# A pre-norm layer of linear attention and a gated bilinear block: the query weights' means taken off by GpSimd in place, three loads moved to ScalarE's queue, two key chunks loaded as one

## The chip, the core and the metric

The kernel runs on one core of one Trainium2 chip. The metric is device microseconds from launch to end, as the median of several runs. The core has five engines that work side by side, each with an instruction stream of its own: TensorE (PE; its weight loads are PEld), VectorE (DVE), ScalarE (ACT), GpSimd (POOL) and SyncE (SP). In this kernel SP does nothing but issue DMAs; ScalarE can issue some too.

## The reference

x is 2048 rows of 640 in bf16. LN takes off a row's mean and divides by its standard deviation.

```python
# 32 heads of 20; softmax over the 20 features of a head, once of p and once of -p
h  = x + A(LN(x))
h2 = h + B(LN(h))

# A: q, k, v = LN(x) @ wqkv, split by heads
pq = einsum("bhsd,hdf->bhsf", q, w_phi);  pk = the same of k
phi_q = concat([softmax(pq), softmax(-pq)]);  phi_k = the same of pk
kv = einsum("bhsf,bhsd->bhfd", phi_k, v);  z = sum over s of phi_k
o  = (phi_q @ kv) / (phi_q . z + 1e-6)
A  = o @ wo

# B: F = 1536
B = ((y @ w_gate) * (y @ w_up)) @ w_down        # y = LN(h)
```

## The kernel before

The 2048 rows are 16 tiles of 128; D = 640 is five chunks of 128 (`NC`). Rows sit on partitions. A row's mean is taken off not from x but from the weights, so that a product with raw x equals one with the centred x; the row's scale `rs` comes later, in the exponential or the evacuation.

**Weights.** Wq, Wk, Wv are the thirds of wqkv. The feature map w_phi is folded into Wk and Wq on the chip: Wk (or Wq) is transposed, and chunk i of the folded matrix is the product of the transposed weights `WT` with the block-diagonal `Phi`. For Wk (`wk_rounds`, units `wk` and `x0` to `x4`) the five chunks are loaded one by one into `Wnat` and transposed by TensorE. For Wq, five DMA transposes (`wqT`, units `t0` to `t4`) write `WT[:, 0]` straight from HBM; `Wnat` then takes plain Wq (unit `lwq`), from which `wq_means` (unit `wm`) computes the mean of each row a of `WT` with small matmuls against `ones`. ScalarE spreads minus the means over 128 columns as `nmu`, a tile that lies in the first buffer of `outb`. `wq_round(i)` (units `y0` to `y4`) then adds two products in one PSUM buffer: six matmuls of `WT` with `Phi`, and six of `nmu` with `Phi`. `evac` writes the sum to `Wp`, by ScalarE for even i, by VectorE for odd. The means of Wk of chunks 2 to 4 are taken off while VectorE and ScalarE evacuate the transposes; for chunks 0 and 1 there is a second product with `nmuk` as above.

**Rows.** 16 DMA transposes of x (`load_xT`; the first four belong to unit `in`, the others are `lT4` to `lT15`) bring `xT`. `stats` (units `s0`, `s2`, `s4`, `s8`, `s12` for the tiles 0-1, 2-3, 4-7, 8-11, 12-15) gets the row sums and, up to tile 11, the sums of squares from matmuls of `xT` with itself; GpSimd turns them into `rs`. Then the units per tile t: `k` projects the keys (ten matmuls of 320 columns), VectorE takes the largest magnitude, ScalarE two exponentials; `K` sums by head (VectorE) and multiplies by the reciprocals (GpSimd, 128x1280); `v` projects the values; `q` and `Q` do for the queries what `k` and `K` do for the keys, and two DMA transposes turn the result. `A0` to `A14` gather keys times values over all tiles in one PSUM buffer, `Aout` writes it to `KVsb`; `n` is the numerator and division, `h` the product with Wo and the residual; `f` the gate and up products, `d` and `e` the down product, the residual and the store.

**Order.** Every piece of work is an operation with its engine, its registers (for the dependences) and its buffers, made by `Prog.op`. The order on each engine is written out in `ORDER`: a list of units per engine, each mention taking that unit's next operation on that engine. `place` walks through the five lists with assumed durations to hand out the buffers of the pools (four PSUM buffers of two banks, three for `eq`, two each for the others) and `finish` sets the semaphores. An engine runs its list strictly in order: what waits holds up everything behind it on that engine. DMAs are issued by SP in its list's order, but for Wrows (w_phi), which ScalarE issues first of all.

Of the kernel before, what the change touches and what calls it, by code (L numbers as in the profile page):

```python
# [5 lines left out]
FP32 = mybir.dt.float32  # L6
# [5 lines left out]
P = 128  # L12
# [60 lines left out]
    "DVE":  # L73
# [12 lines left out]
    "ACT":  # L86
# [9 lines left out]
    "POOL":  # L96
# [37 lines left out]
class Op:  # L134
    __slots__ = ("eng", "idx", "emit", "deps", "dma", "waits", "vc", "signal", "tick", "sem", "val",
                 "n", "dur", "lat", "bufs", "succ", "start", "end", "open", "bytes", "unit")


class Prog:
# [13 lines left out]
    def op(self, eng, emit, rd=(), wr=(), app=(), dma=None, t=0.2, lat=None, use=(), after=(), size=0.0):  # L153
        o = Op()
        o.eng, o.emit, o.dma = eng, emit, dma
# [44 lines left out]
    def place(self):  # L200
# [20 lines left out]
        while len(order) < len(ops):  # L221
# [29 lines left out]
            if o.dma is not None:  # L251
                land = max(s + 2.3, fabric) + o.bytes
                fabric = land
                o.end = land + o.lat
                flight.setdefault(o.dma[0], []).append(o.end)
            else:
                o.end = s + o.lat
# [119 lines left out]
def _build(ctx, nc, A_x, A_wqkv, A_w_phi, A_wo, B_w_gate, B_w_up, B_w_down, out):  # L377
# [43 lines left out]
    nmean = sb([P, NC], FP32, "nmean")  # L421
    Ssum = sb([P, 2, 2 * H], FP32, "Ssum")
# [9 lines left out]
    nmu, nmuk = [outb[:, k, :].rearrange("p (a n) -> p a n", a=NC) for k in range(2)]  # L432
# [31 lines left out]
    def load(out_, in_, wr, mb, after=(), eng="SP", app=()):  # L464
        return g.op(eng, lambda e: e.dma_start(out_, in_), wr=wr, app=app, after=after, dma=("w", 8), t=0.5, lat=0.4, size=mb / 0.38)  # L465

    def transpose(out_, in_, rd, wr, use=(), t=1.27, size=1.07):

        return g.op("SP", lambda e: e.dma_start_transpose(out_(), in_()), rd=rd, wr=wr, use=use, dma=("tr", 8), t=t, lat=0.5,  # L469
                    size=size)  # L470
# [27 lines left out]
    def load_wnat(w, cs=(0, NC), eng="SP"):  # L498
        c0, c1 = cs
        load(Wnat[:, c0:c1, :], A_wqkv[P * c0:P * c1, D * w:D * (w + 1)].rearrange("(c p) n -> p c n", p=P), R_Wnat[c0:c1],  # L500
             0.16 * (c1 - c0), eng=eng)

    def load_xT(t):
        transpose(lambda: xT[:, t, :, 0:P], lambda: A_x[0, P * t:P * (t + 1), :], [], [R_xT[t]], t=1.27, size=0.8 if t < 2 else 1.4)

    def load_x(b):
        load(x_all[:, 4 * b:4 * b + 4, :], A_x[0, 4 * P * b:4 * P * (b + 1), :].rearrange("(t p) n -> p t n", p=P), [R_x[b]], 0.64)

    def load_wv(c0, c1):
        load(Wp[:, c0:c1, 2 * D:3 * D], A_wqkv[P * c0:P * c1, 2 * D:3 * D].rearrange("(c p) n -> p c n", p=P), R_Wp[2][c0:c1], 0.16 * (c1 - c0))  # L510

    U("in")
    load(Wrows[:, :, :], A_w_phi.rearrange("h d f -> (h d) f").rearrange("(a p) f -> p a f", p=P), [R_Wrows], 0.03, eng="ACT")
    for c in range(NC):
        load_wnat(1, (c, c + 1))
    load_wv(0, 2)
# [587 lines left out]
```

## Time and profile before

| | us |
|---|---|
| median of 3 runs (lowest to highest) | 281.2 (280.83 to 281.42) |
| the profiled execution | 281.24 |
| its span, first to last instruction | 279.4 |
| busy: PE, PEld | 274.6, 187.7 |
| busy: DVE, ACT, POOL | 165.5, 133.4, 106.3 |
| DMA: 28.08 MB in 65241 packets | mean 100 GB/s |

The granted TensorE clock is full throughout. Times in the views are microseconds from the start of the span; "x10" behind a group counts its instructions; a bracket "[0.55 <-DVE ...]" is idle time ahead of an instruction and what ended it. L568 is the helper that issues all matmuls, L469 the DMA transposes on SP's queue (SPq), L465 the plain loads, L827 and L857 GpSimd's products of keys and queries, L686 its spreading of Wk's means. The share of the DMA engines counts the time of packets, those that wait included, so that it can exceed 1.

### The profile page before, as it was taken

The numbers are of one execution on the slowest core, as the hardware profiler recorded it, in microseconds if no ns is written. First come the engines' busy times: TensorE is split into PE (matmuls) and PEld (weight loads), VectorE is DVE, ScalarE is ACT, GpSimd is POOL, SyncE is SP. The second block draws the span as 40 slices with busy tenths as digits, with TensorE's granted clock in tenths as the row PEclk, the third lists the DMA queues.
The fourth block names the chain that finished last, engine by engine and source line by source line (L and its number), as shares of the span: only waits on it lengthen the run. The fifth ranks groups of instructions, "written<-read, shape, count | busy, mean of one in ns | idle before, by whom it ended". The sixth has DMA issues, their size and how long they took to land.

```text
span 279.4 us, 5540 instructions
## 1 busy us (share of the span) xinstructions
PE 274.6 (98%) x2257; PEld 187.7 (67%) x2257; DVE 165.5 (59%) x313; ACT 133.4 (48%) x227; POOL 106.3 (38%) x156
## 2 busy tenths in 40 slices
PE   8999999999999999999999999999999999999996
PEld 7777778778878888877746655676454444456773
DVE  2999999999899798688528474431141132315011
ACT  2477999998566346363271432401444342410321
POOL 5348899999620322233300680002521034000321
PEclk9999999999999999999999999999999999999999
DMA  7989989404964378946530065561210001000112
GB/s 192 166 170 140 214 125 397 137 2 94 302 78 94 74 180 150 280 99 91 122 73 2 7 136 72 116 98 45 72 49 0 0 0 49 0 0 2 70 48 72
DMA packets 65241, 28.08 MB, mean 100 GB/s; under 512 B 55744, under 2 KB 63936, under 8 KB 65216
## 3 DMA queue, kind: packets, MB, share of 16 engines
q1 hardware_dynamic: 64560, 27.70, 45.8%
q8 instruction: 18, 0.29, 0.5%
q10 hardware_dynamic: 656, 0.03, 0.2%
q14 instruction: 7, 0.06, 0.1%
HBM read 11.82 MB, written 2.62 MB: 52 GB/s over the span
## 4 chain that ended last, share of the span: by engine, by line
PE 94%; SPq 3%; DMA 2%; DVE 1%; issue 0%
PE ps L568 93%; SPq L469 2%; DMA xT<-in_A_x_dram 2%; SPq L465 1%; PE ps L480 0%; DVE outb L1010 0%; DVE KVsb L893 0%; DVE rden L927 0%; DVE KVsb L896 0%
## 5 line engine op out<-in xcount | busy, mean ns | idle before, releaser
L568 PE MATMUL ps<-phik,Wgu 128*128 128x512 bf16 (+1 forms) x600 | 107.6, 336 | 0.0
L568 PEld LDWEIGHTS ps<-phik,Wgu 128*128 128x128 bf16 x600 | 58.2, 98 | 43.6 <-DVE phik L969 1.2
L969 DVE TENSOR_TENSOR phik<-ps,gate 128x512 bf16<-128x512 f32 (+1 forms) x60 | 34.0, 575 | 61.2 <-PE ps L568 60.3
L568 PE MATMUL ps<-Wp,xT 128*128 128x320 bf16 x480 | 68.4, 299 | 0.0
L967 ACT ACTIVATE gate<-ps 128x512 bf16<-128x512 f32 (+1 forms) x60 | 30.1, 512 | 70.4 <-PE ps L568 56.5
L568 PE MATMUL ps<-vaug,phik 128*128 128x320 bf16 (+3 forms) x544 | 60.2, 270 | 0.0
L568 PEld LDWEIGHTS ps<-Wp,xT 128*128 128x128 bf16 x480 | 46.2, 98 | 17.1
L568 PEld LDWEIGHTS ps<-vaug,phik 128*128 128x128 bf16 x544 | 43.4, 97 | 15.9
L985 POOL TENSOR_TENSOR outb<-t,x_all 128x640 bf16<-128x640 f32 x12 | 16.8, 1397 | 88.0 <-ACT t L982 85.7
L827 POOL TENSOR_TENSOR phik<-phik,Rk 128x1280 bf16<-128x1280 bf16 x16 | 37.3, 2357 | 0.7 <-DVE nb L809 0.6
L982 ACT ACTIVATE t<-ps,mh,rs 128x640 f32<-128x640 f32 x12 | 10.6, 882 | 41.4 <-PE ps L568 41.4
L806 DVE TENSOR_REDUCE ps<-ps 128x1 f32<-128x640 f32 x32 | 26.2, 819 | 3.5 <-PE ps L568 3.1
L846 DVE TENSOR_REDUCE Sq<-eq 128x64 f32<-128x1280 bf16 x16 | 23.5, 1474 | 1.6 <-ACT eq L813 1.6
L824 DVE TENSOR_REDUCE Ssum<-phik 128x64 f32<-128x1280 bf16 x16 | 23.4, 1471 | 0.1
L857 POOL TENSOR_TENSOR eq<-eq,rq 128x640 bf16<-128x640 bf16 x16 | 20.3, 1270 | 0.9
L852 POOL TENSOR_TENSOR rq<-Sq,rq 128x32 f32<-128x32 f32 x16 | 4.0, 255 | 39.8 <-DVE rq L851 39.8
L813 ACT ACTIVATE eq<-ps,nb,rs 128x640 bf16<-128x640 f32 x16 | 14.1, 883 | 10.1 <-DVE nb L809 9.3
L813 ACT ACTIVATE phik<-ps,nb,rs 128x640 bf16<-128x640 f32 x16 | 14.0, 884 | 3.1 <-DVE nb L809 3.0
L561 ACT ACTIVATE junk<-x_all 128x640 bf16<-128x640 bf16 x20 | 14.7, 735 | 0.0
L833 ACT ACTIVATE vaug<-ps,rs 128x640 bf16<-128x640 f32 x16 | 12.8, 801 | 3.5 <-PE ps L568 3.5
L813 ACT ACTIVATE eq<-ps,nb,nrs 128x640 bf16<-128x640 f32 x16 | 14.1, 882 | 0.0
L946 DVE SCALAR_TENSOR_TENSOR x_all<-ps,mh,x_all 128x640 bf16<-128x640 f32 x16 | 13.9, 874 | 0.4
(83 smaller groups left out, 226.4 us busy)
## 6 DMA issues: line engine op xcount, KB each, us to landing
x_all<-in_A_x_dram SPq DMA_DIRECT2D x4, 640.0 KB, 9.0
out_dram<-outb SPq DMA_DIRECT2D x15, 160.0 KB, 1.8
Wgu<-in_B_w_up_dram SPq DMA_DIRECT2D x1, 1920.0 KB, 11.3
Wgu<-in_B_w_gate_dram SPq DMA_DIRECT2D x1, 1920.0 KB, 8.2
vaug<-in_B_w_down_dram SPq DMA_DIRECT2D x1, 1920.0 KB, 8.5
phiqT<-in_A_wqkv_dram SPq DMA_DIRECT2D x5, 160.0 KB, 3.8
phiqT<-in_A_wqkv_dram SPq DMA_DIRECT2D x1, 800.0 KB, 6.0
Wo<-in_A_wo_dram SPq DMA_DIRECT2D x1, 800.0 KB, 5.6
```

Of the source, the lines that this page charges most:

```text
L561: g.op("ACT", lambda e: e.activation(out=junk[:, v.i, :], in_=in_, func=func, accum_out=acc), rd=rd, wr=wr, use=[v], t=0.73, lat=0.97)
L568: ins = e.matmul(o_, lhsT=l_, rhs=r_, start=s_, stop=p_, skip_group_check=True)
L806: g.op("DVE", lambda e: e.tensor_reduce(out=mx(), in_=PS[v.i][:, :, 0:HALF], axis=AX.XY, op=ALU.max, apply_absolute_value=True, negate=Tru ...
L813: g.op("ACT", lambda e, s=s, sc=sc: e.activation(out=signed(dst(), s), in_=PS[v.i][:, :, 0:HALF].rearrange("p b (h f) -> p b h f", f=DH), ...
L824: g.op("DVE", lambda e: e.tensor_reduce(out=Ssum[:, vs.i, :], in_=x, axis=AX.X, op=ALU.add), rd=R_phik[t], wr=vs.R, use=[vs], t=1.39, lat=1.5)
L827: g.op("POOL", lambda e: e.tensor_tensor(out=x, in0=x, in1=Rk[:, vr.i, :].unsqueeze(2).to_broadcast([P, 2 * H, DH]), op=ALU.mult), rd=vr.R ...
L846: g.op("DVE", lambda e: e.tensor_reduce(out=Sq[:, vs.i, :], in_=eq[:, b.i, :].rearrange("p (g f) -> p g f", f=DH), axis=AX.X, op=ALU.add), ...
L857: return e.tensor_tensor(out=x, in0=x, in1=rq[:, vr.i, :].unsqueeze(2).to_broadcast([P, H, DH]), op=ALU.mult)
L946: g.op("DVE", lambda e: e.scalar_tensor_tensor(out=xv, in0=PS[v.i][:, :, 0:HALF], scalar=mh[:, t:t + 1], in1=xv, op0=ALU.subtract, op1=ALU ...
L967: g.op("ACT", lambda e: e.activation(out=gate[:, vg.i, 0:P * n], in_=PS[v.i][:, 0, 0:P * n], func=ACT.Copy), rd=[v.R[0]], wr=vg.R, use=[v, ...
L969: g.op("DVE", lambda e: e.tensor_tensor(out=hhT[:, hb, ft, sl], in0=PS[v.i][:, 1, 0:P * n], in1=gate[:, vg.i, 0:P * n], op=ALU.mult), rd=[ ...
L985: g.op("POOL", lambda e: e.tensor_tensor(out=outb[:, vo.i, :], in0=t32[:, v3.i, :], in1=x_all[:, t, :], op=ALU.add), rd=v3.R + [R_h[t]], w ...
```

## The change

It has three parts and a new `ORDER`.

- `wq_means` writes minus the five means as 128x5 (`nmeanq`) on ScalarE, and five GpSimd instructions (units `wq0` to `wq4`) add column a to `WT[:, 0, a, :]` in place; `wq_round` drops the six matmuls with `nmu`.
- Wq (`lwq`), Wo (`lwo`) and the last quarter of x (`lx3`) are issued by ScalarE: `lx3` and `lwq` behind the evacuation of x4, `lwo` behind `wm`.
- Chunks 2 and 3 of Wk are one load of 320 KB, issued by ScalarE behind Wrows; chunks 0, 1 and 4 stay with SP.
- The lists of all five engines are written anew. Assumed durations in `place` change as well (`at`, `t`, `size`, `lat`); they act on the hand-out of buffers and DMA semaphores alone.

```diff
 ORDER, heads of the lists
 "PE":
-  warm wk x10 x1 wv x1 x0 x3 wv x0 s0 s0 x2 x4 k0 k0 k0 s2 k0 k0 s2 k1 k3 v1 k2 s4 s4 s4 s4
-  k6 k4 v5 k7 v6 k5 v3 s8 s8 s8 s8 k8 v4 wm v11 k9 v10 k10 s12 v7 s12 s12 s12 y4 y0 y1 y3 k11 y2 ...
+  warm wk x10 x1 wv x1 x3 x0 x0 wv s0 x2 k0 s0 k0 x4 k0 k0 s2 k1 s2 k0 k3 s4 s4 s4 s4
+  k6 v0 k4 wm k5 v7 v3 k2 s8 s8 s8 s8 k7 v5 v2 y4 k8 s12 s12 y0 s12 s12 k9 y1 v4 y3 k11 y2 ...
+  ... k15 v9 A0 v13 A2 q2 A2 q3 v15 A4 A4 q5 A6 A6 A8 A8 A10 A12 A14 A10 A12 A14 n0 n1 n1 q6 n1 n0 q7 n0 ...
 "ACT":
-  in wk wk wk in x0 x2 x4 k0 k0 k1 v1 k1 k3 k3 k2 s12 k2 v5 k4 k4 ...
+  in in in wk wk wk x0 x2 x4 lx3 lwq k1 k1 k0 k0 k3 k3 v0 s12 wm lwo k6 k6 s12 v7 k4 v3 k4 ...
 "POOL":
-  ... s4 K1 K0 K3 s8 s8 s8 s8 s8 s8 K2 K4 K6 s12 K5 K8 s12 ...
+  ... s4 s2 K1 wq1 wq2 K3 K0 wq4 s8 wq0 wq3 s8 s8 s8 s8 s8 K5 s4 s12 K6 s12 ...
 "SP":
-  in x11 lT4 lT5 lT7 lT6 lx3 lT8 lT11 lT10 lT9 lT15 t0 lT13 lwq t3 lT12 t2 t4 t1 lT14 lwo lu lx0 lx2 Q0 Q0 ...
+  in x9 lT4 lT6 lT5 lT7 t1 t2 lT8 lT11 lT10 lT9 t3 t4 lT15 t0 lT13 lT12 lT14 lg lx0 lu Q0 Q0 lx2 ...
...
-    for c in range(NC):
-        load_wnat(1, (c, c + 1))
+    load_wnat(1, (0, 1), at=3.0)
+    load_wnat(1, (2, 4), "ACT", at=4.8)
+    load_wnat(1, (1, 2), at=3.7)
+    load_wnat(1, (4, 5), at=5.3)
...
-        g.op("ACT", lambda e: e.activation(out=nmu[:, :, :], in_=PS[v.i][:, 0, 0:NC].unsqueeze(2).to_broadcast([P, NC, P]),
-                                           func=ACT.Copy, scale=-1.0 / SC), rd=[v.R[0]], wr=[R_nmu], use=[v], t=0.61, lat=0.75)
+        g.op("ACT", lambda e: e.activation(out=nmeanq[:, :], in_=PS[v.i][:, 0, 0:NC], func=ACT.Copy, scale=-1.0 / SC),
+             rd=[v.R[0]], wr=[R_nmu], use=[v], t=0.1, lat=0.23)
+        for a in range(NC):
+            U("wq%d" % a)
+            pool_op(lambda e, a=a: e.tensor_scalar(out=WT[:, 0, a, :], in0=WT[:, 0, a, :], scalar1=nmeanq[:, a:a + 1], scalar2=None,
+                                                   op0=ALU.add), 0.75, rd=[R_nmu, R_WT[0][a]], wr=[R_WT[0][a]])
...
-        g.op("PE", lambda e: mms(e, part(WT[:, 0, :, P * i:P * (i + 1)], first) + part(nmu, first)), rd=R_WT[0] + R_Phi + [R_nmu],
-             wr=v.R, use=[v], t=0.62, lat=0.77)
+        g.op("PE", lambda e: mms(e, part(WT[:, 0, :, P * i:P * (i + 1)], first)), rd=R_WT[0] + R_Phi,
+             wr=v.R, use=[v], t=0.31, lat=0.46)
...
-    load_wnat(0)
+    load_wnat(0, eng="ACT")
...
-    load(Wo[:, :, 0:D], A_wo.rearrange("(c p) n -> p c n", p=P), R_Wo, 0.8)
+    load(Wo[:, :, 0:D], A_wo.rearrange("(c p) n -> p c n", p=P), R_Wo, 0.8, eng="ACT")
```

In the heads of the lists "wk x10" and "in x9" count mentions in a row.

More of the change, by code (lines that the diff above doesn't have):

```diff
@@ L135 @@
     __slots__ = ("eng", "idx", "emit", "deps", "dma", "waits", "vc", "signal", "tick", "sem", "val",
-                 "n", "dur", "lat", "bufs", "succ", "start", "end", "open", "bytes", "unit")
+                 "n", "dur", "lat", "bufs", "succ", "start", "end", "open", "bytes", "unit", "at")
 class Prog:
@@ L151, in __init__, with op @@
         self.order = {}
-    def op(self, eng, emit, rd=(), wr=(), app=(), dma=None, t=0.2, lat=None, use=(), after=(), size=0.0):
+    def op(self, eng, emit, rd=(), wr=(), app=(), dma=None, t=0.2, lat=None, use=(), after=(), size=0.0, at=0.0):
         o = Op()
+        o.at = at
         o.eng, o.emit, o.dma = eng, emit, dma
@@ L251, in place @@
             if o.dma is not None:
-                land = max(s + 2.3, fabric) + o.bytes
+                land = o.at or max(s + 2.3, fabric) + o.bytes
                 fabric = land
@@ L421, in _build @@
     nmean = sb([P, NC], FP32, "nmean")
+    nmeanq = sb([P, NC], FP32, "nmeanq")
     Ssum = sb([P, 2, 2 * H], FP32, "Ssum")
@@ L431, in _build @@
     WT = pq[:, NC * D:3 * NC * D].rearrange("p (w a n) -> p w a n", w=2, a=NC)
-    nmu, nmuk = [outb[:, k, :].rearrange("p (a n) -> p a n", a=NC) for k in range(2)]
+    nmuk = outb[:, 1, :].rearrange("p (a n) -> p a n", a=NC)
     vaug = BV[:, :].rearrange("p (t h e) -> p t h e", t=NT, h=H)
@@ L462, in _build, with load, transpose @@
     R_hT, R_oT, R_hhT = [regs(4) for _ in range(2)], [regs(4) for _ in range(2)], [[regs(4) for _ in range(NF)] for _ in range(2)]
[L464 to L470, printed above, removed]
+    def load(out_, in_, wr, mb, eng="SP", at=0.0):
+        return g.op(eng, lambda e: e.dma_start(out_, in_), wr=wr, dma=("w", 8), t=0.5, lat=0.4, size=mb / 0.38, at=at)
+    def transpose(out_, in_, rd, wr, use=(), t=1.27, size=1.07, lat=0.5, at=0.0):
+        return g.op("SP", lambda e: e.dma_start_transpose(out_(), in_()), rd=rd, wr=wr, use=use, dma=("tr", 8), t=t, lat=lat,
+                    size=size, at=at)
     def transpose_pe(out_, in_, rd, wr, use, v, bk):
@@ L494, in U, with load_wnat, load_xT, load_wv @@
         g.unit = name
-    def load_wnat(w, cs=(0, NC), eng="SP"):
+    def load_wnat(w, cs=(0, NC), eng="SP", at=0.0):
         c0, c1 = cs
         load(Wnat[:, c0:c1, :], A_wqkv[P * c0:P * c1, D * w:D * (w + 1)].rearrange("(c p) n -> p c n", p=P), R_Wnat[c0:c1],
-             0.16 * (c1 - c0), eng=eng)
-    def load_xT(t):
-        transpose(lambda: xT[:, t, :, 0:P], lambda: A_x[0, P * t:P * (t + 1), :], [], [R_xT[t]], t=1.27, size=0.8 if t < 2 else 1.4)
+             0.16 * (c1 - c0), eng=eng, at=at)
+    def load_xT(t, at=0.0):
+        transpose(lambda: xT[:, t, :, 0:P], lambda: A_x[0, P * t:P * (t + 1), :], [], [R_xT[t]], t=1.3, size=0.75, lat=1.25, at=at)
     def load_x(b):
-        load(x_all[:, 4 * b:4 * b + 4, :], A_x[0, 4 * P * b:4 * P * (b + 1), :].rearrange("(t p) n -> p t n", p=P), [R_x[b]], 0.64)
-    def load_wv(c0, c1):
-        load(Wp[:, c0:c1, 2 * D:3 * D], A_wqkv[P * c0:P * c1, 2 * D:3 * D].rearrange("(c p) n -> p c n", p=P), R_Wp[2][c0:c1], 0.16 * (c1 - c0))
+        load(x_all[:, 4 * b:4 * b + 4, :], A_x[0, 4 * P * b:4 * P * (b + 1), :].rearrange("(t p) n -> p t n", p=P), [R_x[b]], 0.64,
+             eng="ACT" if b == NB - 1 else "SP")
+    def load_wv(c0, c1, at):
+        load(Wp[:, c0:c1, 2 * D:3 * D], A_wqkv[P * c0:P * c1, 2 * D:3 * D].rearrange("(c p) n -> p c n", p=P), R_Wp[2][c0:c1], 0.16 * (c1 - c0), at=at)
     U("in")
-    load(Wrows[:, :, :], A_w_phi.rearrange("h d f -> (h d) f").rearrange("(a p) f -> p a f", p=P), [R_Wrows], 0.03, eng="ACT")
-    for c in range(NC):
-        load_wnat(1, (c, c + 1))
-    load_wv(0, 2)
-    load_wv(2, 5)
-    for t in range(4):
-        load_xT(t)
+    load(Wrows[:, :, :], A_w_phi.rearrange("h d f -> (h d) f").rearrange("(a p) f -> p a f", p=P), [R_Wrows], 0.03, eng="ACT", at=3.3)
+    load_wnat(1, (0, 1), at=3.0)
+    load_wnat(1, (2, 4), "ACT", at=4.8)
+    load_wnat(1, (1, 2), at=3.7)
+    load_wnat(1, (4, 5), at=5.3)
+    load_wv(0, 2, 6.6)
+    load_wv(2, 5, 8.5)
+    for t, at in enumerate((7.9, 8.5, 10.3, 11.5)):
+        load_xT(t, at)
     def pool_op(f, t, **k):
@@ L1019, in wqT @@
         U("t%d" % a)
-        transpose(lambda: WT[:, 0, a, :], lambda: A_wqkv[:, P * a:P * (a + 1)], [], [R_WT[0][a]], t=1.27, size=1.4)
+        transpose(lambda: WT[:, 0, a, :], lambda: A_wqkv[:, P * a:P * (a + 1)], [], [R_WT[0][a]], t=1.5, size=0.75, lat=1.25)
     U("warm")
```

86 rows, old and new, of the table ORDER are left out of this document.

## The prediction

> **What bounds the kernel now.** I read the chain of waits first, then TensorE's timeline, then the queue that issues DMAs, then GpSimd's groups. The chain of work that ended last, in order of time:
>
> ```profile
> 3.60 0.47 SPq L465
> 4.07 0.04 issue
> 4.12 1.30 SPq L469
> ...
> 9.02 4.64 DMA xT<-in_A_x_dram
> 13.65 0.05 issue
> 13.70 62.00 PE ps L568 x670
> ...
> 76.62 1.91 PE ps L568 x20
> ...
> 85.88 190.10 PE ps L568 x1312
> ```
>
> Up to 13.70 us the end hangs on issues and on the fourth transposed tile of x; from there it is TensorE to 275.99 us, with one gap of 0.55 us before 76.62 (waiting for KVsb). After it 3.4 us of evacuation and store remain. So whatever TensorE is spared behind 13.70 us counts in full, and whatever TensorE is made to wait counts in full too. The same by stretch (columns: PE, PEld, DVE, ACT, POOL busy; clock; DMA share; GB/s):
>
> ```profile
> 14.00:21.00 7.00, 7.00 (x67) 5.37 (x65) 6.52 (x17) 5.25 (x7) 2.81 (x9) 1.00 0.88 171
> 21.00:28.00 7.00, 7.00 (x53) 5.06 (x52) 7.00 (x18) 5.45 (x9) 5.92 (x9) 1.00 1.14 139
> 35.00:42.00 7.00, 7.00 (x72) 5.21 (x71) 6.68 (x10) 6.63 (x11) 6.74 (x3) 1.00 0.90 129
> ```
>
> PE has no hole, but DVE, GpSimd and the DMA engines have few as well: a plan that lets PE run ahead meets them next.
>
> **Part 1: the query rounds y0 to y4.** TensorE's timeline:
>
> ```profile
> 41.84 0.47 PE L568 MATMUL ps<-Phi,phiqT 128*128 128x140 bf16 x6
> 42.15 0.48 PE L568 MATMUL ps<-Phi,outb 128*128 128x140 bf16 x6
> 42.47 0.48 PE L568 MATMUL ps<-Phi,phiqT 128*128 128x140 bf16 x6
> ```
>
> A round is twelve matmuls in 0.63 us (41.84 to 42.47); the six with `outb` (the spread means `nmu`) go. That is 42.47 - 42.15 = 0.32, by five rounds -1.57 us (measured starts, 0.627 to 0.630 a round). PE is full there, so all of it counts. The means' activation on ScalarE falls from 715 ns (128x640) to about the 0.20 us of the 128x1 copies of `wo_mean`: no gain, since ScalarE waits for PE and DVE there.
>
> In exchange GpSimd gets five instructions over 128x640. Nearest rows:
>
> ```profile
> L857 POOL TENSOR_TENSOR eq<-eq,rq 128x640 bf16<-128x640 bf16 x16 | 20.3, 1270 | 0.9
> L686 POOL CAST outb<-nmean 128x640 bf16<-128x640 f32 x1 | 0.7, 716 | 2.6 <-DVE nmean L684 2.6
> ```
>
> The first reads two tiles, the second one; the new instruction reads one tile and one column, so I take 0.72 and keep 1.27: 3.6 us, at most 6.4. What covers it: GpSimd's last key product K15 ends at 72.03 and TensorE's first A14 matmul that reads it starts at 74.01. In the new order K1 comes earlier: when s4's statistics end at 18.0 (below), four sums on DVE (1.0), k3's small product (0.2), K1's reduction (1.48), k6's maximum (0.8) and the reciprocal (0.54) put K1 at about 22.2 instead of 24.85, 2.6 us sooner, and 1.6 us of idle (0.51, 0.52, 0.55) between K1 and K15 can be used. K15 then ends between 72.03 - 2.6 + 3.6 - 1.6 = 71.4 and 73.0, and A14 comes at about 72.6: 0 us taken, 0 to 0.4 kept. Queued behind the new waits: behind wq1 (which waits for the transposed Wq and for `nmeanq`) are wq2, K3 and K0; behind wq0 are wq3 and the row scales of tiles 8 to 11, for which DVE's product of k8 waits.
>
> **Part 2: the start.** SP now issues five loads instead of seven ahead of the transposes, at 0.47 us each: xT0 is issued at 3.18 instead of 4.12. But the bytes are the same, and in the trace xT0 (issued at 4.12) landed at 9.94, after the last value weights (9.14): so its lead lies between 0.3 and 0.94 us. I take 0.8, nearer the issues, because the later tiles land 1.0 to 1.2 us apart with issues every 1.3. On TensorE the order is now x1 wv x1 x3 x0 x0 wv s0 x2 k0 s0 k0 x4 k0 k0 s2 k1 s2 k0 k3 s4. With chunks 2 and 3 landed together x1 starts at 6.9 (7.27 before); the pieces (0.31 a round part, 0.54 and 0.83 for wv, 0.28 a statistic, 0.27 a k0 chunk) bring x4 to 11.2, its evacuation on ScalarE to 12.4 (0.70), k1 to 12.5. The 0.47 us wait for xT3 is filled by k1 (1.36), and s4 could begin at 15.8. Before, with v1 and k2 (2.72) in between, it began at 19.43: a lead of 0.9 us.
>
> **Part 3: s4, where the lead meets the transposes.** The queue of SP and TensorE before:
>
> ```profile
> 4.12 12.38 SPq L469 DMA_TRANSPOSE xT<-in_A_x_dram  x8
> 16.55 0.59 SPq L465 DMA_DIRECT2D x_all<-in_A_x_dram  x1
> 17.18 7.85 SPq L469 DMA_TRANSPOSE xT<-in_A_x_dram  x5
> ```
>
> ```profile
> 13.99 5.60 PE L568 MATMUL ps<-Wp,xT 128*128 128x320 bf16 x40
> 19.43 1.30 PE L568 MATMUL ps<-xT 128*128 128x129 bf16 x20
> 20.56 9.67 PE L568 MATMUL ps<-Wp,xT 128*128 128x320 bf16 x70
> ```
>
> Tiles 4 to 7 landed at 15.17, 16.33, 17.51 and 18.49; s4 used them from 19.43, so they had 0.9 us to spare. With 0.8 us of lead the fourth lands at 17.7 and s4 ends at 17.98 instead of 16.93. Before, at the same work, PE stood at 20.56 - 2.72 = 17.84. The whole lead of the start is used up there: +0.14.
>
> On top of that, `lx3` (a quarter of x, 640 KB) and `lwq` (800 KB) are now issued by ScalarE right behind x4's evacuation, at 12.5 and 13.1, with first packets 1.4 us later as before: while tiles 5 and 7 are still to come. Their issue costs ScalarE 1.2 us, hidden by the 3.0 us that it idles ahead of its first exponential. Their packets (1152 of 1280 B, 55 ns each when the engines are full, over 16 engines) are 3.96 us of DMA work. Between 14.0 and 17.9 us the engines were busy 0.61 to 0.86, about 1 us free, and lx3's own first microsecond moved only about 100 KB; so a start of lx3 fits in, lwq does not need to. I take +0.3, between 0 and 3.96.
>
> **Part 4: the later deadlines.** From 18.3: wm at 18.3 + 3 x 1.36 = 22.4 needs Wq, which took 6.0 us from issue before and now has lx3 (about 3.0 in the queue) ahead: 19.1 to 22.1, 0 taken. s8 at 28.4 needs the sixth transpose after tile 7: 17.7 + 6 x 1.32 = 25.6. y4 at 33.6 needs t0 (four more, 30.9) and two products on GpSimd: 32.4. s12 at 35.3, its third tile at 35.9, needs tile 14 at 34.8. So 1.0 to 2.8 us spare, but six of the 17 later transposes took 1.9 to 2.2 us to issue instead of 1.28: 0 to 1.5 kept. Taking `lx3`, `lwq` and `lwo` off SP saves it 2 us of issue, already in these times. Wo isn't needed before its sums on ScalarE (43.9 before). The orders behind 77 us are new on every engine; PE has no hole there to win, none is visible to lose: 0. The last 3.4 us stay, e15 being last as before.
>
> **Sum.** -1.57 + 0.14 + 0.3 = -1.13 on the profiled 281.24 (span 279.4 and 1.84 around it; the median of the runs is 281.2, the same within their spread of 0.6): 280.1.
>
> **Rivals.** *The loads on ScalarE's queue hold up s4 and wm (slower).* TensorE stops at s4, and perhaps at wm for Wq; ScalarE's wm and the exponentials of k6 stand behind it. For: the DMA share of 0.88 over 14 to 21 us and above 1 after it, with no spare for 4 us; against: the idle shares above. If three quarters of the 3.96 us go ahead of tile 7, 281.24 - 1.43 + 3.0 = 282.8; it makes the kernel slower from 1.4 us on. [...]
>
> *The transposes stay late up to s12 (no change).* Three slow issues between tile 7 and tile 14 (2.2 us) against 1.0 us spare, and GpSimd's wq0 behind t0: +1.2, 281.3.
>
> *GpSimd's five cost 1.27 each (slower).* K15 at 74.2 to 75.8 against A14 at 72.6: about +2, 282.1. Against: the cast row.
>
> *s4 does not wait (faster still).* If tiles 4 to 7 come with the full lead and the loads only fill holes: -1.57 - 0.9 = 278.8.
>
> That the change does not do what it says I exclude for the matmuls: 30 fewer are counted (2227).
>
> **Chances.** Forecast 0.42 (own range 279.5 to 280.6); s4 free 0.12; late up to s12 0.13; loads in the way 0.26; GpSimd dear 0.07. A measurement of this kernel tells about 0.2% (0.56 us) from no change. Faster by more than that: nearly all of the forecast and s4 free, 0.53; within it: most of the third and the forecast's upper edge, 0.16; slower 0.31. The range leaves out the far end of the loads' rival and half of the fastest case: 278.8 to 282.9.
>
> **What would show it.** PE's group with `outb` operands keeps only x0's and x1's twelve matmuls; y rounds 0.32 apart. PE idle at s4 near 16 to 18 us, ended by xT, about 1 us (forecast), 0 (s4 free) or 2 to 4 us (loads in the way, with xT landings spread to 2 us or more). Then no idle at wm, y4, s12 or A14. GpSimd's new group at 0.7 us. A start of s4's last matmul after 19.3 us, or an idle at A14, makes the forecast wrong.

## The result, and the profile after

The changed kernel takes 291.39 us (median of 6 runs, 289.99 to 292.76) against 281.77 (6 runs, 280.83 to 282.79) for the kernel before on the same chip: a ratio of 1.034, 95% interval 1.029 to 1.038. The profiled execution took 291.94 us with a span of 290.2. All of the loss lies ahead of the first numerator: n0 starts at 86.40 us instead of 75.49, and from there both kernels need the same 200 us to TensorE's last matmul.

The chain of waits after, where before there was one piece of 62 us on TensorE (start, length, what):

```profile
14.50 8.18 DMA xT<-in_A_x_dram
22.69 0.05 issue
22.73 6.82 PE ps L573 x60
29.55 0.02 issue
29.58 0.19 ACT nmeanq L730
29.76 0.09 issue
29.86 3.79 POOL phiqT L734 x2
33.64 4.64 POOL phik L836 x2
38.28 1.86 POOL phiqT L734
40.15 0.17 POOL msq L622
40.31 3.73 POOL phiqT L734 x2
44.04 0.04 issue
```

Read it downwards: the eighth tile of x takes 8.18 us from issue to landing, TensorE can only then finish s4, and from 29.86 to 44.04 GpSimd (POOL) sets the pace, without a pause: its five additions (L734) and, between them, the key products K3 and K0 (L836). In this stretch TensorE stood twice, at s4 and at y4 (the bracket is idle time and what ended it):

```profile
22.73 0.46 PE L573 MATMUL ps<-xT 128*128 128x129 bf16 x5 [3.28 <-DMA xT<-in_A_x_dram]
...
44.09 0.50 PE L573 MATMUL ps<-Phi,phiqT 128*128 128x140 bf16 x6 [3.88 <-POOL phiqT L734]
```

and the additions are much dearer than the 716 ns of the cast that the prediction went by:

```profile
L734 POOL TENSOR_SCALAR phiqT<-phiqT,nmeanq 128x640 bf16<-128x640 bf16 x5 | 9.4, 1893 | 0.5 <-ACT nmeanq L730 0.5
```

By stretch (busy time of PE, PEld, DVE, ACT, POOL; granted clock; DMA share; GB/s):

```profile
14.00:21.00 7.00, 5.45 (x57) 4.12 (x55) 5.70 (x19) 3.63 (x5) 4.83 (x14) 1.00 0.92 190
21.00:28.00 7.00, 5.27 (x30) 3.33 (x31) 4.77 (x15) 2.44 (x4) 3.67 (x9) 0.76 1.15 193
...
35.00:42.00 7.00, 5.20 (x50) 3.78 (x47) 6.45 (x17) 5.86 (x8) 7.00 (x5) 1.00 1.09 193
42.00:49.00 7.00, 4.91 (x49) 3.49 (x50) 1.52 (x4) 2.31 (x4) 6.57 (x10) 0.76 1.04 396
```

PE has holes where it had none; GpSimd is full from 35 to 42; and the clock is 0.76 in the stretch behind each hole, which is 3.4 us at half clock (24.0 to 27.4 and 44.4 to 47.8), with matmuls of 320 columns 0.27 us apart instead of 0.136.

The queues show the third thing. While the eighth tile is under way, ScalarE's queue has two big loads of its own:

```profile
q10 hardware_dynamic: 2768, 2.65, 3.6%
...
phiqT<-in_A_wqkv_dram ACTq DMA_DIRECT2D x1, 800.0 KB, 9.6
...
x_all<-in_A_x_dram ACTq DMA_DIRECT2D x1, 640.0 KB, 5.6
```

Queue q10 is ScalarE's (656 packets before). The quarter of x was issued at 14.40 and landed at 20.01; tile 7, issued at 14.50 by SP, landed at 22.69; Wq, issued at 14.81, at 24.36. Between 16 and 18 us the DMA engines served nearly only ScalarE's queue (packets, MB, share of the engines):

```profile
q10 hardware_dynamic: 370, 0.47, 76.4%
q1 hardware_dynamic: 16, 0.00, 0.9%
```

q1 is SP's queue. In the kernel before, with its own eighth tile under way in the same two microseconds, there was no other:

```profile
q1 hardware_dynamic: 913, 0.23, 66.4%
```

### The profile page after: what moved, and what is told of

It reads as the page before. It is cut to its first block, busy times and chain, and to the rows that moved or that the text cites. A ratio compares the mean times of both kernels' runs of the same rounds, so it can differ in the third digit from the quotient of the medians.

```text
span 290.2 us, 5457 instructions
## 1 busy us (share of the span) xinstructions
PE 276.9 (95%) x2214; PEld 188.4 (65%) x2227; DVE 165.7 (57%) x313; ACT 133.3 (46%) x227; POOL 116.4 (40%) x161
## 4 chain that ended last, share of the span: by engine, by line
PE 85%; POOL 5%; SPq 5%; DMA 3%; DVE 1%; issue 1%; ACT 0%
PE ps L573 84%; SPq L471 4%; POOL phiqT L734 3%; DMA xT<-in_A_x_dram 3%; POOL phik L836 2%; SPq L467 1%; DVE Sq L855 1%; PE ps L482 0%; DVE outb L1019 0%; DVE KVsb L902 0%; DVE rq L860 0%; DVE phik L978 0%; ACT nmeanq L730 0%; POOL msq L622 0%; DVE KVsb L905 0%
## 5 line engine op out<-in xcount | busy, mean ns | idle before, releaser
L573 PE MATMUL ps<-phik,Wgu 128*128 128x512 bf16 (+1 forms) x588 | 106.2, 336 | 0.6
L573 PE MATMUL ps<-Wp,xT 128*128 128x320 bf16 x480 | 72.9, 307 | 0.0
L978 DVE TENSOR_TENSOR phik<-ps,gate 128x512 bf16<-128x512 f32 (+1 forms) x60 | 33.6, 574 | 55.1 <-PE ps L573 50.4
L836 POOL TENSOR_TENSOR phik<-phik,Rk 128x1280 bf16<-128x1280 bf16 x16 | 37.5, 2358 | 1.2 <-DVE nb L818 1.0
L961 POOL TENSOR_SCALAR vpe<-shc 128x1 f32<-128x1 f32 x16 | 3.1, 192 | 45.6 <-ACT junk L566 44.7
L822 ACT ACTIVATE phik<-ps,nb,nrs 128x640 bf16<-128x640 f32 x16 | 14.2, 889 | 0.0
```

What stands on the lines that cost most here:

```text
L573: ins = e.matmul(o_, lhsT=l_, rhs=r_, start=s_, stop=p_, skip_group_check=True)
L822: g.op("ACT", lambda e, s=s, sc=sc: e.activation(out=signed(dst(), s), in_=PS[v.i][:, :, 0:HALF].rearrange("p b (h f) -> p b h f", f=DH), ...
L836: g.op("POOL", lambda e: e.tensor_tensor(out=x, in0=x, in1=Rk[:, vr.i, :].unsqueeze(2).to_broadcast([P, 2 * H, DH]), op=ALU.mult), rd=vr.R ...
L978: g.op("DVE", lambda e: e.tensor_tensor(out=hhT[:, hb, ft, sl], in0=PS[v.i][:, 1, 0:P * n], in1=gate[:, vg.i, 0:P * n], op=ALU.mult), rd=[ ...
```

## The experiments

**Theory.** (a) GpSimd's addition costs 1.89 us in this form, and y4 waits for five of them; (b) the loads on ScalarE's queue go ahead of tile 7, so s4 waits; (c) the new order asks for tiles and query weights sooner than the DMA engines can bring them. **Rivals**: the place and not the form makes the addition slow; the joint key chunks delay the start; the clock, halved behind each wait, is a cost of its own; the order has another bound.

### One part undone

`no_means` has part 1 undone (the edit in words):

```diff
-   five units wq0..wq4 on GpSimd; nmeanq 128x5; y rounds of 6 matmuls
+   nmu spread over 128 columns by ScalarE; y rounds of 12 matmuls
```

> The changed kernel with its first part taken back: ScalarE spreads the means as 128x640 again, a query round has twelve matmuls, GpSimd has none of the five additions; order, queues and chunks stay as changed. Theory (GpSimd's price): the five took 1.89 us each, 9.4 us in all, and TensorE waited 3.9 us at y4 for the last of them, with a lower granted clock for some 3 us after it. Then y4 waits for nothing, the clock stays full behind it, and 3.9 + 1 - 1.6 = 3.3 us go: about 288. Rival (y4 would wait for the transposed Wq anyway, which landed at 38.1): about 1.6 us slower than the changed kernel or equal, 291 to 293, with a wait at y4 that a DMA ends.

Measured: 285.82 us, ratio to before 1.016 (1.009 to 1.023). The wait at y4 is gone (y4 at 36.55) though s4 still waited 3.4 us. By the ratios 5.0 us come back, more than expected; the two intervals leave about 2 us either way. The 30 matmuls (1.57 us) are put back in it, so the GpSimd additions would have cost some 6.5 us on their own if those matmuls counted in full, which no run here shows.

`no_queue` has part 2 undone:

```diff
 "ACT": ... x0 x2 x4 [-lx3 lwq-] k1 ... wm [-lwo-] k6
 "SP":  ... lT7 [+lx3 lwq+] t1 t2 ... lT14 [+lwo+] lg
```

> The changed kernel with its second part taken back: the last quarter of x and Wq are issued by SP behind tile 7's transpose, Wo behind tile 14's; the rest stays as changed. Theory (ScalarE's loads take the DMA engines from tiles 5 and 7): tile 7 lands at about 17.5 instead of 22.7, s4 waits 0 to 1 us instead of 3.3, the clock stays full from 21 to 28 us; Wq lands some 6 us behind tile 7, so wm may wait 1 to 2 us, and y4 still waits for GpSimd: about 287 to 289. Rival (tile 7 is late for another reason, an instruction fetch or SP's own queue): s4 still waits 3 us, 291.

Measured: 288.34 us, ratio 1.020 (1.014 to 1.026). Tile 7 lands at 17.73 instead of 22.69. TensorE's gap at s4, from one weight load's start to the next, shrinks from 3.55 to 0.85 us, and measured in the same way wm now waits (1.67 us, for Wq landed at 23.50), s8 (1.08) and y4 (4.53; 4.31 in the changed kernel). GpSimd's run of additions begins 5.2 us sooner (24.64), but its last two now wait for the transpose t0, landed at 36.19. Three to four us come back, not the whole 5 by which tile 7 is sooner.

`no_chunks` has part 3 undone (five single loads on SP):

```diff
-    load_wnat(1, (0, 1)); load_wnat(1, (2, 4), "ACT"); load_wnat(1, (1, 2)); load_wnat(1, (4, 5))
+    for c in range(NC): load_wnat(1, (c, c + 1))
```

> The changed kernel with its third part taken back: five single loads of the key weights on SP. Theory (the joint load shares the engines with the value weights and lands at 6.5 us): the first product x1 starts at about 7.3 instead of 8.5. Whether the 1.2 us reach the end is open: ScalarE's loads follow x4 and go earlier too, so all shifts and 290.2; rival: SP's transposes, one step later in issue, hold s4 at the same time, 291.4.

Measured: 292.62 us, ratio 1.037 (1.034 to 1.040). Undoing it gains nothing; the joint load isn't where the time went.

`order_alone` has all three undone and keeps the new lists (in words):

```diff
 "PE", "DVE", "ACT", "POOL", "SP": as in the changed kernel, but for
+   nmu and 12 matmuls a round; lx3 lwq behind lT7 and lwo behind lT14 on SP; five single chunk loads on SP
```

> The kernel before with the new order alone: all three parts taken back. Theory (the three parts make the loss, each in its place): no wait over 1.5 us at s4, y4 or wm, the clock full, and 282 to 284.5, the s4 and wm waits of 0 to 2 us being what the order costs by itself. Rival (the order asks for the transposed tiles sooner than any queue brings them): 286 or more.

Measured: 285.06 us, ratio 1.010 (1.007 to 1.013). The order alone loses 2.8 us by the ratio. Tile 14 lands at 39.67 and s12 starts at 39.18, where the prediction had 34.8 and 35.3. The expectation had no wait at the start and a full clock; this profile shows 1.6 us of waiting for the first value weights there, and half clock from 8.56 to 11.97. Neither need be the order's: profiles with the start of the kernel before (`before`, `b_dve`, `forms`, `forms2`, `forms3`) wait there for 0 to 1.4 us.

By the ratios the parts undone one at a time give back 5.0, 4.0 and -0.9 us, and all three together 6.7 of the 9.5 us lost.

### What the addition costs, by form

`forms` puts nine instructions into the kernel before, late in its engines' lists (GpSimd's ran at 235 to 243 us, VectorE's at 255), away from the work around y4:

```diff
+    memset; tensor_scalar(t, column) over 640, over 320; tensor_scalar(t, 0.5); tensor_tensor(t, column spread); copy    # GpSimd
+    tensor_scalar(t, column) x2    # VectorE
+    activation(Identity, bias=column)    # ScalarE
```

> The kernel before with nine instructions on a 128x640 bf16 tile put at the end of GpSimd's, VectorE's and ScalarE's work: on GpSimd an addition of a 128x1 column over 640 elements, the same over 320, of the constant 0.5 over 640, of the column as a spread tensor operand, and a copy; on VectorE the column addition twice; on ScalarE an Identity activation with the column as its bias. Its time is not the question, only the durations. Theory 'the column makes the form slow': the column over 640 takes 1.9 us, the constant 0.7 to 1.3. Theory 'GpSimd works at this rate on any tensor_scalar': column and constant both take 1.9, the 320 about 1.0. Rival 'the place, not the form' (GpSimd was slowed by what ran beside it at 30 to 44 us): the column addition takes 0.7 to 1.0 here. VectorE 0.2 to 0.8, ScalarE 0.7 (as its 128x640 copies).

The groups (busy us, mean ns of one, idle ahead):

```profile
L1084 POOL TENSOR_SCALAR Wp<-Wp,mbc 128x640 bf16<-128x640 bf16 x1 | 1.9, 1908 | 0.1
L1084 POOL TENSOR_SCALAR Wp<-Wp 128x640 bf16<-128x640 bf16 x1 | 1.8, 1808 | 0.1
...
L1088 POOL TENSOR_TENSOR Wp<-Wp,mbc 128x640 bf16<-128x640 bf16 x1 | 1.3, 1252 | 0.1
L1084 POOL TENSOR_SCALAR Wp<-Wp,mbc 128x320 bf16<-128x320 bf16 x1 | 1.1, 1090 | 0.1
...
L1089 POOL COPY Wp<-Wp 128x640 bf16<-128x640 bf16 x1 | 0.7, 716 | 0.1
```

```profile
L1084 DVE TENSOR_SCALAR Wp<-Wp,mbc 128x640 bf16<-128x640 bf16 x2 | 0.8, 382 | 0.0
```

It is the form, not the place and hardly the column: tensor_scalar on GpSimd over 128x640 takes 1.81 us with a constant and 1.91 with a column; by the two lengths that is 2.6 ns an element and 0.27 us fixed (an estimate: 1908 - 1090 over 320 elements). The same sum as a tensor_tensor with the column spread takes 1.25, a copy 0.72, VectorE 0.38, ScalarE 0.81. The two rows that the prediction took as its ends, a copy and a tensor_tensor, were both cheaper forms.

### The additions on VectorE

`a_dve` is the changed kernel with the five additions on VectorE, spread over its list from 30 to 38.6 us:

```diff
-            pool_op(lambda e, a=a: e.tensor_scalar(out=WT[:, 0, a, :], ...
+            g.op("DVE", lambda e, a=a: e.tensor_scalar(out=WT[:, 0, a, :], ...
```

> The changed kernel with the five additions on VectorE instead of GpSimd, spread over 30 to 38.6 us; nothing else changed. Theory 'GpSimd's 9.4 us are what y4 waits for and what the slow clock behind it comes from': y4's wait of 3.9 us falls to below 0.6, the clock stays full there, 285.8 less up to 1.57: 284.3 to 286.5. Rival 'y4 waits anyway, for t0 landed at 38.1': y4 at 38.6 to 39, wait 0 to 1.5 us, 286.5 to 288.5.

Measured: 285.9 us, ratio 1.013 (1.010 to 1.017). The profile has no wait at y4 (37.55), none at s12, and full clock from 13.29 on; hence GpSimd's form costs the changed kernel up to 5.5 us. Up to, because s4 did not wait in this profile either: x4's evacuation came late, so ScalarE issued its loads at 16.05, 1.45 us behind tile 7, which landed at 18.23. So the start decided whether the loads caught tile 7: in the changed kernel, with the first of them issued 0.10 us ahead of it (14.40 and 14.50), they did; here they did not. But what is left, 1.3%, cannot be told from the 1.6% with part 1 undone, so a gain from the 30 matmuls isn't shown. TensorE comes to y4 4 us behind the forecast's 33.6: s4 begins at 19.95 instead of 15.8, and TensorE stands 0.9 us in front of v2, for ScalarE.

`b_dve` is the kernel before, orders kept, with part 1 alone and its additions on VectorE:

```diff
 "DVE": ... k9 K6 k9 [+wq0 wq3 wq2+] K8 [+wq4+] k10 [+wq1+] K5 k10 s12 ...
```

> The kernel before with part 1 alone and the five additions on VectorE instead of GpSimd (three behind k9's maximum, one behind K8's sums, one behind k10's maximum); orders else as before. y rounds lose 30 matmuls, 1.57 us. Theory 'the idea is sound and only GpSimd's price spoilt it': VectorE's additions at 0.3 to 0.8 us each fit ahead of 41.8 us and K15 has 2 us of slack: 280.0 to 280.6 against 281.6. Rival 'TensorE only runs into the next wait' (VectorE is 95% busy there, so K7 to K15 all come later): s12, y's evacuations or A14 wait by as much: 281.4 to 283.

Measured: 285.75 us, ratio 1.016 (1.011 to 1.020), slower than both theories allowed. Two waits stand out besides 1.4 us at the start: 0.8 us at wm for Wq, and 2.5 us at y4 for VectorE. VectorE's additions (shortest/median/longest ns) and the GpSimd product beside them:

```profile
L730 DVE TENSOR_SCALAR phiqT<-phiqT,nmeanq x5: 374/375/2482, 40.6 to 46.0; 128x640 bf16<-128x640 bf16 x5
```

```profile
40.78 2.44 POOL L832 TENSOR_TENSOR phik<-phik,Rk 128x1280 bf16<-128x1280 bf16 x1 [0.41 <-DVE nb L814]
```

The long one starts at 40.93, just behind the start of GpSimd's K6, and ends at 43.41, just behind its end at 43.23. In `a_dve` one addition took 1.29 us in the same way, ending at 30.29 behind K3's end at 30.11. To test that, `forms3` lets GpSimd do five spread-column additions while VectorE does its own on another tile (`forms2`, the first attempt, missed: GpSimd's instructions ran at 235 us and VectorE's at 255, and gave only VectorE's prices alone, 0.39 for the column addition and 0.82 for the tensor addition).

> The kernel before with instructions put at its end, for their durations alone: GpSimd does five tensor additions of a spread column (1.25 us each) on one 128x640 bf16 tile, while VectorE, beside them on another tile, does an addition of the same kind, a column addition (tensor_scalar), another of each, and two more column additions. Theory 'VectorE's column addition, 0.37 us alone, cannot run while a GpSimd instruction runs, and ends just behind it': each column addition that starts during a GpSimd instruction ends 0 to 0.25 us behind that one's end, and VectorE's tensor addition keeps a fixed duration of its own. Rival 'the 2.48 and 1.29 us seen with the additions on VectorE had another cause': 0.37 to 0.45 each beside GpSimd.

> The kernel before with instructions put at its end, for their durations alone, this time at the same moment: GpSimd's five tensor additions (1.25 us each, back to back) and VectorE's tensor addition (0.82 alone), column addition (0.39 alone), another of each, and two more column additions. Theory 'VectorE's column addition cannot run beside a GpSimd instruction and ends just behind it': each column addition ends 0 to 0.25 us behind the end of a GpSimd addition, and the tensor addition keeps about 0.8. Rival: 0.37 to 0.45 each.

```profile
255.02 7.68 POOL L1087 TENSOR_TENSOR Wp<-Wp,mbc 128x640 bf16<-128x640 bf16 x5 [19.54 <-DVE mbc L1084]
```

```profile
254.98 0.83 DVE L1094 TENSOR_TENSOR Wp<-Wp,mbc 128x640 bf16<-128x640 bf16 x1
255.84 1.26 DVE L1091 TENSOR_SCALAR Wp<-Wp,mbc 128x640 bf16<-128x640 bf16 x1
257.13 1.79 DVE L1094 TENSOR_TENSOR Wp<-Wp,mbc 128x640 bf16<-128x640 bf16 x1
258.96 3.92 DVE L1091 TENSOR_SCALAR Wp<-Wp,mbc 128x640 bf16<-128x640 bf16 x3
```

Every column addition takes 1.26 to 1.29 us beside GpSimd, against 0.39 alone: the first ends at 257.10, 0.19 us behind GpSimd's first instruction (256.91). The part on the tensor addition failed: the second took 1.79 instead of 0.8, and GpSimd's own ran up to 1.89 instead of 1.25. So on VectorE the additions that met a GpSimd instruction were dear, 1.26 to 1.29 us here and in `a_dve`, 2.48 in `b_dve`, where the other four took 0.37 to 0.38; and GpSimd pauses little: in the kernel before it is at work for 6.74 of the 7 us from 35 to 42.

### Part 3 alone

`b_chunks` is the kernel before with the joint key chunks:

```diff
-    for c in range(NC): load_wnat(1, (c, c + 1))
+    load_wnat(1, (0, 1)); load_wnat(1, (2, 4), "ACT"); load_wnat(1, (1, 2)); load_wnat(1, (4, 5))
```

> The kernel before with part 3 alone: chunks 2 and 3 of the key weights in one load issued by ScalarE, SP with five loads ahead of the transposes; all orders else as before. The prediction's step says 0.3 to 0.9 us of lead for the first transpose, and with s4's spare tiles the time falls by up to 0.9: 280.7 to 281.4. The theory from the trace of the changed kernel says that the joint load lands at about 6.5 and all bytes are the same, so x1 starts no sooner and later by up to 1.2 us: 281.6 to 282.8.

Measured: 282.69 us against 282.13, ratio 1.001 (0.997 to 1.004): the gain of 0.9 us isn't there, and a loss of 1 us isn't shown either. The profiles of all kernels tell what it does at x1: with single loads x1 starts at 6.92 to 7.66 (eight profiles, mean 7.18), with the joint one at 6.96 to 8.89 (eight, mean 8.04).

### What the new order waits for

`no_wqT` is `order_alone` without the five transposes of the query weights; its y rounds read the transposed key weights, so it leaves the query weights out of the result:

```diff
 "SP": ... lT7 lx3 lwq [-t1 t2-] lT8 lT11 lT10 lT9 [-t3 t4-] lT15 [-t0-] lT13 lT12 lT14 ...
-   part(WT[:, 0, :, ...], first)
+   part(WT[:, 1, :, ...], first)
```

> The new order alone, without the five transposes of the query weights on SP's queue: the y rounds read the transposed key weights instead, so the query weights are left out of the computation. Theory 'the transposes set the pace of the new order': in every kernel so far with that order the last two tiles of x land at 38.1 to 39.8 us, and s12 starts at 39.2 to 39.5; with five of the 13 transposes behind tile 7 gone, at 1.5 us each, they land at about 32, the waits at y4 (0.62) and s12 (0.91) go, and so does whatever of the start's losses those waits would have swallowed: 281.0 to 283.6 against 285.1. Rival 'the new order has a bound of its own' (VectorE or GpSimd): the waits turn up elsewhere, 284.3 to 285.3.

Measured: 283.56 us, ratio 1.004 (1.001 to 1.006): 1.8 us better than `order_alone` by the ratios. Tile 14 lands at 33.40, and the stretch that holds y4 and s12 fills up (`no_wqT` first, `order_alone` second):

```profile
35.00:42.00 7.00, 7.00 (x92) 5.72 (x90) 6.37 (x11) 6.39 (x11) 5.72 (x7) 1.00 1.04 398
```

```profile
35.00:42.00 7.00, 6.32 (x81) 4.71 (x80) 5.34 (x7) 5.46 (x9) 5.56 (x9) 1.00 1.06 166
```

So the transposes cost the order about two thirds of its 2.8 us. The rest is 1.0 us. That is a bound from one side: the kernel before has the five transposes too, and was not run without them.

`stream_first` is `a_dve` with two loads moved behind the transposes, and `after_late` the changed kernel with the same move; they ask whether the loads slow the transposes:

```diff
 "SP":   ... lT12 lT14 [+lx3 lwo+] lg lx0 ...
 "ACT":  ... x4 [-lx3-] lwq ... v0 [-s12-] wm [-lwo-] k6 k6 [-s12-] v7 ... y0 [-s12-] k8 k8 s12 v4 [+s12+] k9 [+s12+] y2 [+s12+] k9 ...
 "POOL": ... K6 [+K7+] s12 s12 s12 [-K7-] s12 K4 ...
```

> The changed kernel with the five additions on VectorE, and with the last quarter of x and Wo (640 and 800 KB) taken off ScalarE's queue and issued by SP behind the last transpose; ScalarE's four sums of squares over that quarter, and GpSimd's row scales for it, come later by as much. Theory 'the DMA engines are full up to 40 us, so what is loaded ahead of the transposes delays them': t0 and tile 14 land 3 to 4 us sooner than with the additions on VectorE alone (34.5 and 38.1 us there), y4 and s12 follow by 1.5 to 3.5 us, 282 to 284 against 285.9; at best as fast as the kernel before or a little faster. Rival 'the pace is that of SP's issues, 1.3 us and more for each': landings move by less than 1.3 us, 285 to 286.

Measured: 284.74 us, ratio 1.006 (1.003 to 1.010), against 1.013 for `a_dve`. t0 lands at 32.99 and tile 14 at 36.39, 1.6 and 1.7 us sooner: more than the rival allowed, half of what the theory wanted. TensorE's waits:

```profile
PE ps L572 <- DMA xT<-in_A_x_dram: 1.3, 1, 1.3
PE ps L572 <- ACT phik L821: 0.9, 1, 0.9
PE ps L572 <- ACT vaug L841: 0.6, 1, 0.6
PE ps L572 <- DVE nb L817: 0.3, 1, 0.3
```

None is at y4 or s12 any more; s4 still waits, now behind Wq alone on ScalarE's queue, and ScalarE's exponentials and evacuations come late. This is the best version of the new order that computes the whole result, and it is not faster than the kernel before.

> The same move of the two loads, with the additions left on GpSimd. Theory 'y4 comes at t0's landing plus three GpSimd additions, and all behind it shifts with it': t0 lands 3 to 4 us sooner than in the changed kernel (38.1 there), y4 as much, 287.5 to 288.5 against 291.4, and the difference to stream_first, 4 to 6 us, is the price of GpSimd's form. Rival 'pace of the issues': 290.5 to 291.5.

Measured: 289.89 us, ratio 1.024 (1.019 to 1.030). t0 lands at 33.73, 4.4 us sooner than in the changed kernel, but y4 comes only 1.9 us sooner (42.15). Both theories missed that GpSimd has its own chain, which runs on without a gap and does not wait for t0:

```profile
25.60 2.35 POOL L835 TENSOR_TENSOR phik<-phik,Rk 128x1280 bf16<-128x1280 bf16 x1
27.94 3.78 POOL L733 TENSOR_SCALAR phiqT<-phiqT,nmeanq 128x640 bf16<-128x640 bf16 x2
31.69 4.67 POOL L835 TENSOR_TENSOR phik<-phik,Rk 128x1280 bf16<-128x1280 bf16 x2
36.34 1.88 POOL L733 TENSOR_SCALAR phiqT<-phiqT,nmeanq 128x640 bf16<-128x640 bf16 x1
38.19 0.20 POOL L621 TENSOR_TENSOR msq<-sm 128x4 f32<-128x4 f32 x1
38.36 3.74 POOL L733 TENSOR_SCALAR phiqT<-phiqT,nmeanq 128x640 bf16<-128x640 bf16 x2
```

It starts when s4's statistics are there, and its length, 16.6 us of instructions, then sets y4. The difference to `stream_first` is 1.8%, 5 us: the price of GpSimd's form, as with `a_dve`.

### The clock

`warm_waits` puts throw-away matmuls into the two waits of the changed kernel:

```diff
+    36 matmuls 128x128 of ones ahead of s4's fourth statistic, 36 ahead of y4
```

> The changed kernel with 36 idle matmuls (128x128, thrown away) put ahead of s4's fourth statistic and 36 ahead of y4, inside the two waits of 3.3 and 3.9 us. Theory 'TensorE's clock is halved because it stood idle': no half-clock stretch behind the two waits, mean clock 1.0 instead of 0.988, and the 1.6 and 1 us that the slow stretches cost come back: 288.5 to 289.3 against 291.4. Rival 'the clock falls for another reason, or the work behind the waits is bound by other engines anyway': 291 to 292.

Measured: 291.02 us, ratio 1.031 (1.027 to 1.034), within the interval of the changed kernel. The two stretches:

```profile
21.00:28.00 7.00, 6.43 (x81) 4.97 (x79) 5.09 (x16) 4.08 (x8) 3.98 (x9) 1.00 1.33 199
42.00:49.00 7.00, 5.80 (x60) 4.26 (x61) 2.47 (x5) 3.29 (x6) 6.57 (x10) 0.76 1.03 393
```

At s4 it worked: 0.84 us between two weight loads were left of 3.55, the clock stayed at 1.00 and k6 to wm took 4.00 us instead of 5.67. At y4 3.10 us were left and the clock fell all the same. But y4 came only 0.9 us sooner (43.20), since GpSimd's chain from s4's statistics sets it: about 0.5 is GpSimd's wait for `nmeanq`, which is gone, and 0.3 an earlier tile 7 (22.37). So filling the wait kept the clock up, and the first halving was worth about 0.5 us of its 1.6. The second one, behind y4, was not undone here. One of the four runs had a mean clock of 0.999 and still took 290.12 us, within the range of the changed kernel.

## Why the prediction was wrong, step by step

The forecast put n0 at 75.49 - 1.13 = 74.36; it came at 86.40, 12.0 us later. On the chain that the runs have shown, s4 to GpSimd to y4 to n0, this is 4.7 + 5.8 (y4 at 44.08 instead of 33.6) + 1.6 (from y4 to n0). Along TensorE the middle piece is 1.9 us of its own work (1.7 of them half clock) and 3.9 us of waiting at y4.

**Part 1, the matmuls: right.** y4's six matmuls take 0.32 us (44.09 to 44.41), half a round. But the 1.57 us count only if the rounds' inputs are there; in no version of this study did they show in the time.

**Part 1, GpSimd: the largest term, mis-sized and misplaced.** 0.72 us was taken and 1.27 kept; 1.89 was measured, so that five cost 9.4 us instead of 3.6 (+5.8). That this equals the 5.8 above is chance: with additions of 0.72 us the same chain would have ended at about 38.2, and TensorE, there at 40.2, would not have waited (an estimate from these rows). The cover was sought at K15 and A14, 30 us behind; the first reader of the additions is y4. The prediction gave y4 1.2 us of slack by counting GpSimd's work from t0's landing; the chain begins at s4's statistics and holds K1, K3 and K0 too. The rival "GpSimd's five cost 1.27 each" had the right engine, at two thirds of the price and the wrong place, and a chance of only 0.07. Bounds from the nearest rows failed because both rows were another form of instruction; an unmeasured form on a slow engine deserved an open upper end.

**Part 2, the start: mis-sized.** x1 was to start at 6.9 and s4 at 15.8; they started at 8.46 and 18.30. In the seven profiles with this start s4 began between 15.93 (`no_queue`) and 19.95 (`a_dve`), 17.9 in the mean: the forecast was the good end. Most of the spread is TensorE's pace. x1 and the matmuls behind it, in the changed kernel and in `no_queue`:

```profile
8.49 0.81 PE L573 MATMUL ps<-Phi,phiqT 128*128 128x140 bf16 x6
9.09 1.27 PE L573 MATMUL ps<-Wp,ones 128*128 128x320 bf16 x4
```

```profile
6.99 0.48 PE L572 MATMUL ps<-Phi,phiqT 128*128 128x140 bf16 x6
7.31 0.71 PE L572 MATMUL ps<-Wp,ones 128*128 128x320 bf16 x4
```

Six matmuls take 0.60 us from start to start in the one and 0.32 in the other. The trace's clock records begin, with a full clock, at 10.30 in the changed kernel, at 3.84 in `no_queue`, and at 6.24 in the kernel before (the text ahead of the prediction calls it full throughout, which it is not); ahead of that the matmuls run at half pace: in the kernel before, five transposes of a key chunk take 0.49 us from start to start (5.76 to 6.25), the next five, behind it, 0.27 (6.38 to 6.65). Of the 2.37 us between the two at s4, 0.96 is the joint load (TensorE had it at 6.52 instead of 5.56) and 1.35 the pace. Whether the change delays the full clock isn't shown: it came at 3.8 to 13.3 us with the joint load, at 3.7 to 10.2 with single ones. The profiles of single loads differ by 2 us too (x1's second half at 7.73 to 9.79), and the forecast stood on one of them, whose 7.99 was near the good end.

**Part 3, s4: the rival's mechanism.** The forecast had 1.35 us of idle in s4, and TensorE stood 3.28 (3.55 between the starts of its weight loads). s4 ended at 22.97 instead of 18.3 (+4.7), of which 2.5 is its later start. "+0.3, between 0 and 3.96" was mis-sized: without the loads on ScalarE's queue (`no_queue`) the gap is 0.85 us, so they put 2.7 on it. The transfers of both queues were under way at once, and not served evenly: the quarter of x landed at 20.01, ahead of tile 7 at 22.69, though the two had been issued at the same moment (14.40 and 14.50), and between 16 and 18 us it was 370 packets of ScalarE's queue against 16 of SP's. The rival's 282.8 was far too low, since it priced the wait alone and not GpSimd's work behind it.

**Part 4, the deadlines: wrong, and readable before.** Tile 14 was to land at 34.8 and landed at 40.29. Thirteen transposes at 1.32 us were counted behind tile 7; in the trace of before the same thirteen, with lx3 and Wq between them, had taken 40.15 - 18.49 = 21.66 us. In the changed kernel they took 17.6, but behind a tile 7 that came 5.0 us late; with tile 7 in time (`no_queue`) 21.8, so tile 14 came at about the same moment (39.54). The rival "late up to s12" held the mechanism at 1.2 us; `order_alone` against `no_wqT` shows 1.8.

**What no step held.** The half clock behind a wait of TensorE: it is the whole of the last 1.6 us. k8, behind y4, in the changed kernel and in `a_dve`, which has the same list on TensorE and full clock there:

```profile
44.41 2.84 PE L573 MATMUL ps<-Wp,xT 128*128 128x320 bf16 x10
```

```profile
37.99 1.52 PE L573 MATMUL ps<-Wp,xT 128*128 128x320 bf16 x10
```

From y4's start to k9's TensorE takes 4.05 us (44.09 to 48.14) against 2.49 (37.68 to 40.17). And the 2.8 us of the order as such, which was costed at nothing because TensorE had no hole to win or lose; 1.0 us of it stays unexplained by the transposes.

## What to carry to other kernels

Before work is put on another engine, measure that very form there, or leave the upper end open: on GpSimd a tensor_scalar cost 2.6 times a copy of the same tile (1.89 us against 0.72). Then find the first reader of the result and follow the receiving engine's own queue from its last wait to that reader; slack further down the kernel does not help. When a plan asks for transfers sooner, hold it against the landing times that the trace shows for the same transfers, not against issues at their shortest. And take a start from several profiles: here s4's moved by 4 us between profiles with the same list.

## What the runs showed of the hardware

GpSimd's tensor_scalar over 128x640 bf16 takes 1.81 to 1.91 us, longer than its tensor_tensor with the same column spread (1.25). VectorE's column addition, 0.38 us alone, took 1.26 to 1.29 us beside GpSimd's additions of 1.25 to 1.89 (`forms3`) and 2.48 beside a product of 2.44 (`b_dve`). The granted clock fell to half for 3.4 us in or just behind gaps between TensorE's weight loads of 3.1 to 4.3 us and for 6.8 us at gaps of 4.5 (`no_queue`) and 5.4 (`after_late`), but not at one of 3.62 in `no_means`; and near the start it fell for 3.4 us with gaps of only 1.9 (`order_alone`, from 8.56) and 1.8 (`warm_waits`, from 8.66): the length alone doesn't decide it, and what else does isn't shown. A transpose issued by SP at the same moment as a big load of ScalarE landed 2.7 us behind that load (22.69 and 20.01).
